# Attention and channel mix on one core: four batches instead of two turned on TensorE, a fourth output buffer, a new written order

## The chip, the core and the metric

The kernel runs on one core of a Trainium2 chip. The metric is the device time of one execution in microseconds. Before the change the median of three runs is 286.31 us (286.21 to 286.6). Five engines work side by side, each in its own written order: TensorE (PE in the profile; its weight loads PEld), VectorE (DVE), ScalarE (ACT), GpSimd (POOL), and SyncE (SP), which here issues every DMA. They wait for each other through semaphores.

## What is computed

Eight batches of eight heads, 576 tokens, 64 channels per head. First attention with a mask by blocks of 64 tokens, then a channel mix in which each token is blended with the token before it:

```python
scores = scale * np.matmul(q, k.transpose(0, 1, 3, 2))
mask = block_i >= block_j                       # blocks of 64 tokens
attn = exp(where(mask, scores, -1e9) - max)     # rows then divided by their sum
x = (attn @ v) -> (B, S, H * D)
xk = mu_k * x + (1.0 - mu_k) * x_prev           # x_prev: x one token earlier
xr = mu_r * x + (1.0 - mu_r) * x_prev
k = np.maximum(xk @ w_k, 0.0)                   # 512 -> 1024
v = k * k @ w_v                                 # 1024 -> 512
out = sigmoid(xr @ w_r) * v
```

## The kernel before

**Tasks and order.** The kernel lists some 1,370 tasks, each bound to one engine (or to one of several, which the string `PLACE` chooses), and then emits them in the sequence of the string `ORDER`. A number in `ORDER` is a task; "+n" after it puts n matmuls on the identity (L270, read by nobody) ahead of a TensorE task. So the order on every engine, and on SyncE's DMA queue, is written out by hand, and each engine runs its list strictly from front to back. A task that waits holds everything behind it on its engine. Buffers are rings with fixed sizes in `RINGS`: a task that takes a buffer waits until the last reader of its former content is done. Among them are "ld" (8, loads of queries, keys and weights), "qkt" (2, turned queries and keys of a batch), "m" (2 banks of PSUM, t_m), "mm" (2 banks of PSUM, t_mm), "s" (2, scores) and "o" (3, output tiles t_o).

**Attention of a batch.** Scores need queries and keys with channels on the partitions, and there are two ways to get them. Batches below `LONGS`, here two, take the *long* way (`add_long`, `add_long_qkt`): one DMA brings two heads, each partition reading a row of nine tokens (2304 bytes); a cast to bf16 by GpSimd, VectorE or ScalarE; groups of nine turning matmuls on TensorE (L391) into a bank t_m; and a copy out of it into t_qkt by ScalarE or VectorE. The other batches take the *DMA* way (`add_qk`): a load of two heads by token rows (256 bytes) in two DMAs (L242), a cast into NB, a tail with the last 64 tokens, loaded and cast by itself, and a DMA transpose (L322) that turns one pair of heads into t_qkt. The scores of a pair are matmuls from t_qkt (L503); exponentials on ScalarE (L525) write t_e; memsets put zeros where the mask cuts (L533); products with values and with ones (L585) go into t_m, four heads at a time; VectorE transposes and inverts the sums and multiplies (L606 to L650) into XT, channels on partitions.

**Channel mix.** Over all tokens there are nine chunks of 512. For each, blends on VectorE and ScalarE or GpSimd (L669 to L704), eight groups of four matmuls with w_k (L732) with rectifier (L744, L746) and square (L754, L756), four groups with w_r (L771) and tanh on ScalarE (L779), four groups of eight matmuls with w_v (L798), the output multiply on VectorE (L809) from t_t and t_mm into t_o, and a store of t_o (L817). The multiply takes one of the three buffers t_o, so it waits for the store three multiplies earlier to land. Channel mix of early batches is interleaved with attention of later ones.

**Queue.** Loads, tail loads, DMA transposes and stores all stand in SyncE's one list. A DMA transpose waits there for its casts, and what stands behind it waits too.

Of the kernel before, what the change touches and what calls it, by code (L numbers as in the profile page):

```python
# [10 lines left out]
BF = mybir.dt.bfloat16  # L11
AF = mybir.ActivationFunctionType
ALU = mybir.AluOpType

LONGS = 2

ORDER = """
0 3 5 7 9 11 4 13 6 17 69+88 8 73 70 15 10 74 173 71+18 12 75 72 19 14 76
85+11 97 86 81 77 53 82 16 98 25 88+9 78 18 174 89 100+11 87 83 27 79 84 101
113+2 23 20 80 90 114 109+11 102 99 21 110 94+11 115 116 26 189 28 95 121+11  # L20
112 111 127+3 122 96 169 125 24 131 126 106+7 1 123 124 54 91+3 22 31 107
128+9 39 129 92 132 37 108 133 103 170 175 117+2 104 93 2 65 134 118 55 105
135 136 40 130+28 32 171 119 120 149 38 138+2 183 137 142 139+5 181 154 151
140+2 143 152 177 176 144 179 156 145 172 29 66 153 146 158 195+31 56 147 67
182 196 197+7 185 184 178 198 199+7 200 150 209+7 35 211 210 155 205 30 45
212 201+2 206 47 180 202 141+11 213 33 68 157 207 289 214 148 36 49 208 159
203+17 215 46 57 204 48 186 160 61 216+20 190 41 34 220 164 217 187 163 165
50 221+30 219 168 43 967 167 222 191 58 973 218 62 162 42 968 223 290 974
969 970 188 166 161 975 976 224 59 44 193 971 226 977 972 314 988 225 192
978 227 985 51 989 230 228 229 63 979 60 291 990 320 194 232 231 986 980 247  # L30
315 233 292 987 982 251 235 234 248 981 298 250 64 252 236 237 238 52 983
253 310 294 321 993+2 239 254 984 997 304 241 240 255 257 249 994 242 293
296 274 243 998 256 995 244 295 1005 277 269 246 245 275 996 322 271 259 276
272 308 258 297 1006 1008 300 299 262 302 263 270 264 324 323 301 1009 1002
325 265 309 327 423 266 326 311 312 261 303 1003 260 313 328 268 305 991 306
267 999 992 307 273 278 284 279 280 1004 283 285 1007 281 1011 402 286 1000
282 1023 403 1012 329 1024 421 1014 333 1013 330 1026 287 316 288 1015 331
334 332 1025 1016 1032 318 335 1027 404 1020 337 1028 431 336 1033 422 339
1021 338 1034 407 1029 429 317 424 340 425 1039 427 343 1022 341 319 1030
345 342 344 417 1040 360 1031 346 361 364 435 1017 348 347 365 405 366 363  # L40
367 1018 350 351 428 432 349 411 430 1041 352 368 370 362 415 436 354 1019
353 356 1037 1042 369 409 355 357 382 1049 387 524 358 359 383 384 385 371
1038 1010 416 406 372 1001 388 1046 375 408 410 1050 412 373 413 426 1047
1035 418 376 389 377 1043 1036 419 1048 378 420 390 379 437 380 374 1044 438
414 1052 386 381 440 392 391 1045 441 395 528 397 396 394 393 1051 398 518
442 401 1055 400 443 1053 433 399 446 1058 444 445 529 439 540 447 1056 1059
1057 1067 1060 448 534 1061 1068 450 449 542 1076 1062 434 451 1070 1069
1077 1054 541 452 536 1078 1063 1079 1071 535 453 544 1064 1080 543 455 1065
454 1072 516 1073 456 1066 473 515 537 1074 458 457 477 1075 474 546 459 475
478 479 1087 461 460 480 522 517 545 463 481 482 519 530 538 464 520 462 532  # L50
476 465 495 521 547 1085 1088 467 466 497 469 1096 498 523 468 1089 496 470
539 483 531 1086 471 472 526 484 1097 525 533 485 500 488 550 489 486 490
551 491 527 1083 502 553 552 501 1093 493 1084 631 503 492 554 1081 629 1094
487 499 1082 504 641 555 505 494 1090 510 559 1098 508 556 628 511 513 630
560 647 512 632 1091 1129 561 558 642 514 643 1125 1130 507 562 563 509 1127
637 645 506 1126 565 564 557 1128 1099 635 648 566 651 1105 1100 569 548 568
567 1117 644 1101 653 633 1106 571 570 1118 659 586 574 1107 1108 636 590
1119 1095 575 1120 572 638 1092 549 634 1109 577 1121 576 573 654 639 587
1122 1110 589 660 578 741 591 1102 592 593 580 646 579 582 1114 594 1103 596
583 1111 1104 581 1115 640 613 588 585 1112 584 597 595 649 1113 663 614  # L60
1116 598 616 664 601 1140 756 602 666 603 665 604 748 608 600 667 605 1141
599 760 607 650 1123 610 609 1131 652 1124 612 615 606 749 1142 1134 617
1132 623 762 761 611 1137 764 744 618 624 1135 626 1133 621 668 1138 661
1167 669 622 742 763 619 1173 672 1168 670 673 1139 627 1174 620 1143 754
674 671 625 662 1161 752 1144 657 676 675 1146 1145 743 1162 750 678 677
1147 746 1149 1163 682 745 1136 1164 1148 679 655 658 1150 684 755 747 1165
1158 687 758 680 757 681 1171 685 1151 751 766 699 1159 1166 688 656 690 689
1172 753 703 1160 700 691 1152 704 686 705 683 693 692 706 759 695 701 696
694 707 767 1155 708 1153 765 697 702 698 1154 1156 721 710 709 776 867 714
1157 711 722 777 712 726 869 1175 715 779 729 778 716 727 770 717 780 781  # L70
723 1181 772 785 1176 868 718 728 782 1177 719 713 863 870 1182 784 786 783
771 720 1169 787 873 724 1178 725 789 788 730 857 731 1170 790 736 791 1179
854 1184 734 795 732 1180 737 874 740 855 792 796 1187 739 773 1185 793 768
797 1188 794 735 1205 871 1189 733 875 800 1199 1206 798 801 812 774 738 856
887 1208 1200 816 858 1183 877 1190 859 802 861 769 1209 1207 803 1201 876
1193 860 804 1191 775 1210 813 806 1192 815 878 1194 808 817 805 807 818
1196 1195 799 819 809 1202 872 820 822 862 811 814 810 1203 864 839 823 865
821 1186 1197 889 827 866 824 1198 890 840 826 1213 892 1204 879 891 834
1222 893 1214 828 836 883 837 835 1211 829 1223 885 894 830 1212 1219 895
842 1224 880 831 833 898 888 896 884 841 881 897 899 1220 825 900 886 1217  # L80
1221 832 902 901 1228 1218 903 882 904 1229 1215 908 1230 1225 838 905 909
843 1216 906 907 849 844 910 1226 925 1227 850 913 926 845 929 1231 911 853
915 1234 930 914 847 1232 931 848 916 1235 932 1249 1236 1233 917 1246 933
912 919 852 921 918 851 927 1250 1247 928 922 1251 934 1259 935 1248 923
1237 947 1260 920 1243 948 1238 950 949 1252 1239 1244 1245 924 1240 846
1253 952 937 1241 936 1254 1242 1255 953 1261 940 1256 941 1269 955 1262 942
954 943 1263 944 1270 1271 938 1264 939 945 1265 1257 946 1266 951 1258 956
957 962 1272 1267 958 1268 965 963 966 1275 1273 964 1293 1274 1276 960 959
1290 1294 1277 1278 1291 1295 961 1303 1292 1279 1296 1304 1280 1281 1297
1298 1284 1282 1287 1283 1285 1286 1305 1288 1289 1299 1306 1316 1300 1313  # L90
1317 1318 1307 1314 1315 1301 1308 1310 1309 1302 1345 1311 1319 1312 1346
1334 1320 1321 1331 1335 1340 1336 1332 1333 1322 1341 1342 1328 1323 1324
1325 1329 1337 1330 1326 1327 1343 1338 1339 1347 1344 1354 1348 1351 1355
1356 1357 1352 1353 1349 1358 1360 1359 1350 1363 1361 1362 1364 1365
"""

PLACE = (
    "PPAPDPPPPPPDDPADPDPPDAPAPAADDAAAAAAAADDDDPPPDDPDPDPDPDPDDAADDDADAPDPAA"
    "AADADDAADDAAPPDPDDPDDDDDDPDPAPDAADAAPAPPDDPDDDDPAPPPDDPPDPPPPPPDPDAPAD"
    "APPDDDDDAPDDDAAPDPDDDPPPDDPDPPDPDAADPPDAAAAPDPDAADAPPPDDDPPDPDPPPPDPPA"  # L100
    "AAAAAAPPPPDDPADADDPPDPDDDDDPPPPPDDDDADPAPDAAPDPDPPPDPDPAPDPPPPDPDPDPDD"
    "PPPDPAPDAAAAAAAPPDDPAAPDDPPPDPPDDDPPDDPDDDAPAAAADPDPAPAPDPDDDDAPADDDDD"
    "DPAPDAAADPDADDDAAAAADPDPAPDDAADADADADDADDPADAADADPAPDAAADDAAAPAADDDDAD"
    "ADAAADAPAADAAPADADAPAPADADAPADADADADADAPADAPADAD"
)


class Plan:

    def __init__(self, rings):
        self.rings = {n: [k, []] for n, k in rings.items()}
        self.tasks = []

# [27 lines left out]
def kernel(  # L144
# [26 lines left out]
    assert S == 576 and D == 64 and C == 512  # L171
    ISQ = float(1.0 / (D ** 0.5))
    PSUM = bass.MemoryType.PSUM

    RINGS = {"ld": 8, "vl": 4, "nl": 4, "nb": 4, "tl": 1, "qkt": 2, "e": 4,
             "xt": 2, "tt": 1, "rc": 2, "rt": 2, "d": 2, "xk": 3, "xr": 2,
             "kr": 3, "k2": 1, "t": 3, "o": 3, "s": 2, "m": 2, "mm": 2,
             "vo": 2, "el": 2}
    plan = Plan(RINGS)
    pools = {}  # L180
    for n, bufs in RINGS.items():
        if n in ("vo", "el", "nb", "xt"):
            continue
# [40 lines left out]
    for i in range(2):  # L224
        nc.vector.memset(VOs[i][D:P, 4], 0.0)
        nc.vector.memset(E4s[i], 0.0)
    for nb in NBs:
        nc.gpsimd.memset(nb[D:P, :, 4], 0.0)

# [170 lines left out]

                def ev(eng, me, y=y, n=n, take=take):
                    qkt = tiles["qkt", b]
                    if take:
                        nc.gpsimd.memset(qkt[:, :, 1, S:KP], 0.0)
                    pst = tiles["pq", b, g, y, n][:, :].bitcast(BF)
                    convert(eng, qkt[:, 2 * g + y, n, 0:S].rearrange(
                                "q (p j) -> q p j", j=JT),
# [504 lines left out]
```

## Time and profile before

| | |
|---|---|
| median of three runs | 286.31 us (286.21 to 286.6) |
| profiled execution | 286.77 us |
| its span, first to last instruction | 285.0 us |
| mean granted clock of TensorE | 0.975 |
| PE / DVE / ACT / POOL busy | 267.1 / 214.7 / 202.4 / 81.5 us |
| DMA queue | 50.88 MB in 137,072 packets, 81.8% of 16 engines |
| DMA transposes | 24, median 4.8 us from issue to landing |
| identity matmuls (L270) | 367, 26.8 us |

Shares are averages over a span whose stages differ: DMA is busy to about 215 us and nearly idle after, and the identity matmuls lie before 42 us. In a line of the timeline the bracket names the idle time of the engine just before and what ended it. A line of windows has, for a stretch, its length, the busy time of PE, PEld, DVE, ACT and POOL, the granted clock of TensorE, the DMA share and GB/s.

### The profile page before, as it was taken

To read this page: it belongs to the slowest core of one execution; us is meant where nothing else is said; L and a number is where in the kernel's file an instruction comes from. 1 tells how busy PE (TensorE), PEld (TensorE's weight loads), DVE (VectorE), ACT (ScalarE), POOL (GpSimd) and SP (SyncE) were. 2 spreads that over 40 slices of the span, in tenths; PEclk is the share of its full clock that TensorE was granted. 3 is DMA by queue.
4 is the path that set the end of the run, shared out by engine and by line. 5 is a ranking of instruction groups with operands and counts; after the bars stand their busy time and mean duration, and the time that the engine had idled before them with its cause. 6 is when DMAs were issued, how large, how long until landed. Compare 5 with 4: busy or idle time off the path is not lost.

```text
span 285.0 us, 8296 instructions
## 1 busy us (share of the span) xinstructions
PE 267.1 (94%) x3351; PEld 132.7 (47%) x3351; DVE 214.7 (75%) x468; ACT 202.4 (71%) x296; POOL 81.5 (29%) x161
## 2 busy tenths in 40 slices
PE   8999999998599977999999989989999999999995
PEld 8866773443234422434444434433454444444443
DVE  1448899798578893598888888999996898952432
ACT  2799599964289365987989599979967991461530
POOL 4421334723053011430163028222133212150110
PEclk9999999999699995999999999999999999999999
DMA  7979899999949998979999999999998201202103
GB/s 219 301 181 335 252 290 247 221 169 201 236 89 195 215 256 207 217 152 180 237 229 155 209 251 227 183 225 234 194 198 183 77 2 39 110 0 96 54 29 118
DMA packets 137110, 51.40 MB, mean 180 GB/s; under 512 B 127728, under 2 KB 127984, under 8 KB 137072
## 3 DMA queue, kind: packets, MB, share of 16 engines
q1 hardware_dynamic: 137072, 50.88, 81.8%
q8 instruction: 26, 0.43, 0.6%
q14 instruction: 12, 0.10, 0.1%
HBM read 33.56 MB, written 9.44 MB: 151 GB/s over the span
## 4 chain that ended last, share of the span: by engine, by line
PE 34%; ACT 15%; DMA 9%; DVE 7%; SPq 6%; issue 3%; POOL 0%; ACTq 0%; DVEq 0%
PE t_mm L732 13%; PE t_mm L798 9%; ACT t_e L525 7%; PE t_mm L771 5%; SPq L242 4%; PE t_m L585 4%; DMA t_qkt<-NB 4%; DMA out_dram<-t_o 3%; PE t_s L503 3%; DVE t_o L809 2%; ACT t_d L669 2%; ACT t_kr L744 2%; SPq L322 2%; DMA t_ld<-in_k_dram 1%; ACT NB L253 1%
## 5 line engine op out<-in xcount | busy, mean ns | idle before, releaser
L525 ACT ACTIVATE t_e<-t_s 128x1024 f16<-128x1024 f32 x96 | 94.2, 1023 | 9.6 <-PE t_s L503 9.5
L732 PE MATMUL t_mm<-t_xk,WK 128*128 128x512 f16 x288 | 73.1, 397 | 7.1 <-DVE t_o L809 6.0
L798 PE MATMUL t_mm<-WV,t_k 128*128 128x512 f16 (+1 forms) x296 | 66.9, 374 | 0.0
L732 PEld LDWEIGHTS <-WK 128*128 128x128 f16 x288 | 27.0, 100 | 44.0 <-issue 19.0
L779 ACT ACTIVATE t_t<-t_mm 128x512 f32<-128x512 f32 x36 | 21.3, 600 | 31.3 <-PE t_mm L771 29.5
L798 PEld LDWEIGHTS <-t_k 128*128 128x128 f16 x296 | 27.9, 98 | 32.7 <-issue 2.2
L809 DVE SCALAR_TENSOR_TENSOR t_o<-t_t,t_mm 128x512 f32<-128x512 f32 (+1 forms) x37 | 24.7, 668 | 22.5 <-PE t_mm L798 12.8
L756 POOL TENSOR_TENSOR t_k<-t_kr 128x512 f16<-128x512 f32 x23 | 25.3, 1104 | 48.8 <-ACT t_kr L744 32.3
L503 PE MATMUL t_s<-t_qkt 64*128 64x64 bf16 (+4 forms) x384 | 34.0, 282 | 3.9 <-DMA t_qkt<-NB 2.3
L771 PE MATMUL t_mm<-WR,t_xr 128*128 128x512 f16 x144 | 36.3, 380 | 1.0 <-DVE t_o L809 1.0
L533 POOL MEMSET t_e<- 64x128 f16 x68 | 13.1, 200 | 69.9 <-ACT t_e L525 57.8
L744 ACT ACTIVATE t_kr<-t_mm 128x512 f32<-128x512 f32 x44 | 26.3, 598 | 8.4 <-PE t_mm L732 8.3
L585 PE MATMUL t_m<-t_e,VO 128*32 128x64 f16 (+4 forms) x1024 | 29.5, 248 | 0.6 <-DVE t_tt L606 0.6
L270 PE MATMUL t_mm<-identb 128*128 128x128 bf16 x367 | 26.8, 227 | 1.4 <-POOL identb masks.py:199 1.4
L746 DVE TENSOR_SCALAR t_kr<-t_mm 128x512 f32<-128x512 f32 x28 | 19.2, 686 | 10.0 <-PE t_mm L732 9.8
L756 DVE TENSOR_TENSOR t_k<-t_kr 128x512 f16<-128x512 f32 x28 | 20.4, 734 | 7.5 <-ACT t_kr L744 7.1
L503 PEld LDWEIGHTS <-t_qkt 64*128 64x128 bf16 x384 | 13.4, 95 | 26.8 <-issue 18.3
L270 PEld LDWEIGHTS <-identb 128*128 128x128 bf16 x367 | 22.0, 102 | 4.7 <-issue 2.6
L585 PEld LDWEIGHTS <-VO 128*32 128x32 f16 x1152 | 17.8, 95 | 12.5 <-issue 7.1
L650 DVE TENSOR_TENSOR XT<-t_m,t_rt 128x512 f32<-128x512 f32 x32 | 21.7, 684 | 0.8 <-PE t_m L585 0.7
L259 POOL CAST NB<-t_ld 128x512 bf16<-128x512 f32 x20 | 13.9, 700 | 24.3 <-DMA t_ld<-in_q_dram 21.0
L771 PEld LDWEIGHTS <-t_xr 128*128 128x128 f16 x144 | 12.6, 97 | 17.1 <-issue 4.7
(59 smaller groups left out, 302.0 us busy)
## 6 DMA issues: line engine op xcount, KB each, us to landing
out_dram<-t_o SPq DMA_DIRECT2D x35, 256.0 KB, 3.0
t_vl<-in_v_dram SPq DMA_DIRECT2D x32, 256.0 KB, 4.9
t_ld<-in_q_dram SPq DMA_DIRECT2D x48, 128.0 KB, 3.7
t_ld<-in_k_dram SPq DMA_DIRECT2D x48, 128.0 KB, 3.4
t_ld<-in_q_dram SPq DMA_DIRECT2D x8, 288.0 KB, 4.9
t_ld<-in_k_dram SPq DMA_DIRECT2D x8, 288.0 KB, 5.7
t_ld<-in_moe_w_v_dram SPq DMA_DIRECT2D x8, 256.0 KB, 5.8
t_ld<-in_moe_w_k_dram SPq DMA_DIRECT2D x8, 256.0 KB, 5.0
```

The source lines that it names most:

```text
L270: nc.tensor.matmul(spare.get("at", dst), identb, identb, start=True, stop=True)
L503: nc.tensor.matmul(PS[:, h, col:col + n], qkt[rows, pr, 1, kc * P:kc * P + P], qkt[rows, pr, 0, q0:q0 + n], start=True, stop=True)
L525: nc.scalar.activation(tiles["e", b, pr][:, :, i, :], tiles["ps", b, it], AF.Exp, scale=ISQ)
L585: nc.tensor.matmul(PA[j * QC:(j + 1) * QC, col + a - lo:col + hi - lo], weight(b, (g, j), kc, kk), moving(b, (g, j), kc, a, hi), start=(kc ...
L650: nc.vector.tensor_tensor(xt[:, 2 * g + "AB".index(kind), 1:1 + CH], PA[:, 0:CH], rt_[:, 0:CH], ALU.mult)
L732: nc.tensor.matmul(ps, WK[:, cc, jc * P:(jc + 1) * P], tiles["xk", c][:, cc], start=(cc == 0), stop=(cc == CCn - 1))
L744: nc.scalar.activation(kt, ps, AF.Relu)
L756: (nc.vector if eng == "DVE" else nc.gpsimd).tensor_tensor(dst, KR, KR, ALU.mult)
L771: nc.tensor.matmul(ps, tiles["xr", c][:, cc, jt * P:(jt + 1) * P], WR[:, cc], start=(cc == 0), stop=(cc == CCn - 1))
L779: nc.scalar.activation(tiles["t", c, jt], tiles["pr", c, jt], AF.Tanh, scale=0.5)
L798: nc.tensor.matmul(ps[:, 0:w], tiles["k2", c][:, jc, jt * P:(jt + 1) * P], WV[:, jc, cols], start=(jc == 0), stop=(jc == JCn - 1))
L809: nc.vector.scalar_tensor_tensor(tiles["o", c, jt, half][:, 0:w], tiles["t", c, jt][:, cols], 1.0, tiles["pv", c, jt, half][:, 0:w], ALU.a ...
```

## The change

`LONGS` goes from 2 to 4: batches 2 and 3 are loaded by nine-token rows and turned on TensorE, and only batches 4 to 7 use the DMA transposes. The ring "o" has four buffers. The pads of the two t_qkt buffers, 64 columns that nobody else writes on the long way, are set to zero once at the start on GpSimd, instead of in the first copy of each long batch. `ORDER` and `PLACE` are new throughout.

```diff
-LONGS = 2
+LONGS = 4
 
 ORDER = """
-0 3 5 7 9 11 4 13 6 17 69+88 8 73 70 15 10 74 173 71+18 12 75 72 19 14 76
...
+0 3 5 13 7 4 9 6 17 69+64 43 73 70 74 15 8 19 10 71+39 75 72 11 44 76 85+11
...
 PLACE = (
-    "PPAPDPPPPPPDDPADPDPPDAPAPAADDAAAAAAAADDDDPPPDDPDPDPDPDPDDAADDDADAPDPAA"
...
+    "PPDDPDDPDPAPDAAPPADPPDADAAADADADADAAAADADDPPDDPDPPPPDDDDPDAAPAAAAAPAAD"
...
@@ RINGS @@
-             "kr": 3, "k2": 1, "t": 3, "o": 3, "s": 2, "m": 2, "mm": 2,
+             "kr": 3, "k2": 1, "t": 3, "o": 4, "s": 2, "m": 2, "mm": 2,
@@ start @@
+    for _ in range(RINGS["qkt"]):
+        nc.gpsimd.memset(new("qkt", [P, HP, 2, KP], BF)[:, :, 1, S:KP], 0.0)
     for nb in NBs:
         nc.gpsimd.memset(nb[D:P, :, 4], 0.0)
@@ add_long_qkt, ev @@
                     qkt = tiles["qkt", b]
-                    if take:
-                        nc.gpsimd.memset(qkt[:, :, 1, S:KP], 0.0)
                     pst = tiles["pq", b, g, y, n][:, :].bitcast(BF)
```

What the two written orders hold, counted by task, where they differ:

| | before | after |
|---|---|---|
| loads by nine-token rows (one DMA each) | 16 | 32 |
| loads by token rows (two DMAs each) | 48 | 32 |
| tail loads (two DMAs each) | 6 | 4 |
| DMA transposes | 24 | 16 |
| turning groups on TensorE (nine matmuls) | 16 | 32 |
| copies out of t_m into t_qkt: ScalarE, VectorE | 8, 8 | 17, 15 |
| identity matmuls | 367 | 401 |
| rectifiers: ScalarE, VectorE | 44, 28 | 50, 22 |
| squares: ScalarE, VectorE, GpSimd | 21, 28, 23 | 19, 26, 27 |

## Prediction

> **What bounds the kernel now.** I read the page first: engine shares, the forty slices, the list of costly groups. Then the waits, then the timeline around the two largest gaps of TensorE, then a table of windows.
>
> ```profile
> span 285.0 us, 8296 instructions
> PE 267.1 (94%) x3351; PEld 132.7 (47%) x3351; DVE 214.7 (75%) x468; ACT 202.4 (71%) x296; POOL 81.5 (29%) x161
> PE   8999999998599977999999989989999999999995
> PEclk9999999999699995999999999999999999999999
> DMA  7979899999949998979999999999998201202103
> L525 ACT ACTIVATE t_e<-t_s 128x1024 f16<-128x1024 f32 x96 | 94.2, 1023 | 9.6 <-PE t_s L503 9.5
> L732 PE MATMUL t_mm<-t_xk,WK 128*128 128x512 f16 x288 | 73.1, 397 | 7.1 <-DVE t_o L809 6.0
> t_qkt<-NB SPq DMA_TRANSPOSE x24, 4.8
> ```
>
> TensorE is busy 94% of the span, so the end is set by its work and its gaps. The gaps are few: the slices show the clock fall twice, in slices 11 and 16, and group L732 says why: 6.0 of its 7.1 us of idle time ended with L809, the output multiply on VectorE. The DMA row is full up to slice 30 and then nearly empty, so loads, stores and DMA transposes fill the queue for three quarters of the span.
>
> The view of waits gives the same chain in two links, an output buffer that waits for a store and TensorE that waits for the output multiply:
>
> ```profile
> PE t_mm L732 <- DVE t_o L809: 6.0, 2, 3.7
> DVE t_o L809 <- DMA out_dram<-t_o: 4.9, 3, 2.9
> ```
>
> The timeline of both places (start, us, engine) shows what held the store: it stands on SyncE's queue behind the DMA transposes (L322), which wait for their casts.
>
> ```profile
> 65.58 3.94 SPq L322 DMA_TRANSPOSE t_qkt<-NB  x2
> 69.56 1.18 SPq L817 DMA_DIRECT2D out_dram<-t_o  x2
> 73.36 0.69 DVE L809 SCALAR_TENSOR_TENSOR t_o<-t_t,t_mm 128x512 f32<-128x512 f32 x1 [2.87 <-DMA out_dram<-t_o]
> 74.10 1.86 PE L732 MATMUL t_mm<-t_xk,WK 128*128 128x512 f16 x4 [3.71 <-DVE t_o L809]
> ...
> 99.85 3.11 SPq L322 DMA_TRANSPOSE t_qkt<-NB  x2
> 105.10 0.26 PE L503 MATMUL t_s<-t_qkt 64*128 64x64 bf16 x6 [1.15 <-DMA t_qkt<-NB]
> 108.62 1.87 PE L732 MATMUL t_mm<-t_xk,WK 128*128 128x512 f16 x4 [2.27 <-DVE t_o L809]
> ```
>
> The windows (span, busy us of PE, PEld, DVE, ACT, POOL, granted clock, DMA share, GB/s) price what follows a gap, and cut the span in stretches that I use below:
>
> ```profile
> 75.00:80.00 5.00, 5.00 (x25) 1.75 (x25) 3.21 (x8) 2.10 (x3) 0.88 (x2) 0.55 1.14 227
> 110.00:115.00 5.00, 5.00 (x20) 1.75 (x19) 2.07 (x4) 3.41 (x5) 1.24 (x2) 0.63 0.90 218
> 5.00:10.00 5.00, 5.00 (x106) 4.69 (x104) 0.75 (x1) 1.91 (x4) 1.69 (x4) 1.00 0.98 348
> 40.00:60.00 20.00, 19.45 (x285) 9.56 (x282) 17.69 (x42) 19.42 (x29) 9.99 (x14) 1.00 1.10 233
> 42.30:128.10 85.80, 76.51 (x878) 32.45 (x877) 67.36 (x151) 60.91 (x89) 27.49 (x50) 0.92 0.99 201
> 128.10:285.00 156.90, 150.50 (x1679) 68.45 (x1677) 121.41 (x254) 110.09 (x166) 39.64 (x73) 1.00 0.71 147
> ```
>
> After each gap TensorE works at about half clock: at 0.55 and 0.63 of it in five full us.
>
> **The change part by part.** The sum stands against the profiled execution: 286.77 us, of which 285.0 are the span and 1.77 lie around it. The median of the runs is 286.31, so 0.46 lower. I cut the span at 42.3 (first matmul of L732) and 128.1 (last exponential of the fourth batch).
>
> *Fourth output buffer, and stores that are not held.* The stalls cost: at 70 us a gap of 3.7, a shorter one of 0.5, and 5.45 us of work at half clock (2.7 lost): 6.9. At 105 us gaps of 0.35, 1.15 and 2.27 and 5 us at half clock (2.5): 6.3. Together 13.2. In the written order of before, at these two places the store stands 0.9 and 1.2 us of TensorE work ahead of the multiply that takes its buffer again. In the new order with four buffers the smallest such distance while loads are running is 4.1 us (last store of chunk 3), the next 9.4, and batches 2 and 3 have no DMA transposes at all. I take both stalls as gone. What is late next is ScalarE, below.
>
> *Loads of batches 2 and 3.* Removed: 16 loads in two DMAs each (1.17 us of queue, the median in the timeline), 2 tail loads (1.33), 8 DMA transposes (1.73): 35 us of SyncE's queue, which is back to back from 41 to 214 us. Added: 16 single loads at 0.43: 7 us. The bytes of queries and keys stay, 4.7 MB, and 2.6 MB of transposes go. At 233 GB/s (40 to 60 us) the old 7.3 MB are 31 us; at 348 (5 to 10 us, when long rows are loaded) the new 4.7 are 14. So queue and DMA engines have 17 to 28 us less to do. None of it is on TensorE's path by itself; it shows as fewer late loads.
>
> *TensorE.* Added are 16 groups of nine turning matmuls. Two groups in a row take 0.60, a single one 0.43, less 0.17 of overlap: 0.21 to 0.26 each, 3.4 to 4.2 us (6.9 if none overlaps; I take 3.4), all of them after the first L732. A group waits for two casts and for one of the two banks t_m, which the copies out free; scores, L585 and L732 queue behind it. Fill matmuls are 401, not 367; 23 of the 34 lie ahead of 42.3, at 0.056 us 1.3, and two score tasks fewer stand there (1.0). So the first stretch is 42.3 + 0.3 = 42.6 (bounds 41 to 45, as the loads come in another order).
>
> *ScalarE.* Nine more copies of turned blocks (0.54 back to back), seven of them up to the last exponential of the fourth batch. In that stretch the order also puts there two exponentials (0.90 each back to back: two take 1.94, one 1.02), three long casts (0.57), three value and two weight casts (0.5), one narrow exponential (0.5), and takes away four items of 0.5. That is 3.8 + 1.8 + 1.7 + 2.5 + 0.5 - 2.0 = 8.3 more. From the window row: 60.9 + 8.3 = 69.2 us of ScalarE. TensorE in the same stretch: 76.5 less 5.2 of half clock is 71.3; four groups of L732 fewer (0.86), one of L771, two of L798 (1.73), two of L585 (0.66) and sixteen turning groups and 11 fills more: 71.3 - 4.1 = 67.2. Before, the stretch without its stalls was 72.6, which is 1.3 over its longer engine. Now two engines are nearly equal, and each runs in order; I take 2.8 over the longer one: 69.2 + 2.8 = 72.0, bounds 69.2 and 82 (the old share, 72.6 us for 60.9 of ScalarE, on 69.2).
>
> *The rest.* What the stretch no longer does comes later: 4 of L732 (3.5), 1 of L771 (0.9), 2 of L798 (3.5), 2 of L585 (1.3): 9.1. The rest was 156.9; with 9.1 it is 166.0. It had 6.4 idle, and its matmuls of L732 take 0.94 instead of 0.86 start to start. With 14 DMA transposes instead of 15 here but 17 instead of 24 split loads, and transposes issued 9 to 38 us of TensorE work ahead of their scores (4 to 22 before), I take 3.0 of it back, bounds 0 and 8: 163.0.
>
> *Pads.* Two memsets of 0.32 on GpSimd move to the start, behind those that end at 2.44; GpSimd waits until 3.79 for the first load, so they cost nothing, and 0.6 if that load came at once. VectorE has slack: ten fewer tail casts, seven more copies, six fewer rectifiers net to some 3 us less of 214.7.
>
> Sum: 42.6 + 72.0 + 163.0 = 277.6, and 1.8 around it: 279.4; less 0.46, 278.9. That is 7.4 us under the profiled execution, 2.6%.
>
> The median issue of a transpose is 1.73 us for 0.33 MB, of a split load 1.17 for 0.26 MB: 5.3 against 4.5 us per MB. [...]
>
> **The rivals.** *ScalarE does not hold* (faster still): the stretch is 69.2 and the late loads go entirely: 42.6 + 69.2 + 158.0 + 1.8 - 0.5 = 271. For it: the larger distances above. Against: in 40 to 60 us ScalarE is already busy 19.4 of 20.
>
> *The stall only moves*: one store or transpose is late again once, with its half clock: 278.9 + 6.6 = 285.5, no real change. For it: 16 transposes remain. Against: the distances.
>
> *Slower*: the copies out of turned blocks stand in ScalarE's full queue, two banks t_m serve both turning and L585, and TensorE, behind a turning group of batch 2 or 3 (45 to 75 us), waits. A wait with its half clock costs some 6.6; two make 278.9 + 13.2 = 292. From 7.4 us of such waits on it decides. For it: 69.2 against 67.2, and ScalarE's windows at 5.0 of 5.0. Against: the new order has 0.5 to 2.3 us of TensorE work between group and copy.
>
> The second drop of the clock came after gaps of 1.15 and 2.27 us with 2 us of work between. [...]
>
> **How the numbers follow.** The forecast has 0.58, the faster rival 0.14, the moved stall 0.13, the slower one 0.11, anything else that slows 0.04. 0.2%, 0.6 us, is about what a measurement tells from no change. Faster: 0.58 + 0.14 and half of the moved stall, 0.79; same 0.06; slower 0.15. The bounds give 41 + 69.2 + 158 + 1.3 = 269.5 at the low end; the high end is the moved stall and a little, 287 (all upper bounds at once, 45 + 82 + 166 + 1.3, would be 294). Out of it are the slower cases and part of the fastest.
>
> **What would show it.** Right: no wait of L809 for a store over 1 us before 215; a granted clock of 1.00 between 45 and 215; the last exponential of batch 3 near 115 us; 16 transposes; ScalarE at 95% between 43 and 115. Wrong: TensorE waiting for turned copies or exponentials over 2.3 us, a clock of 0.5 in any window of that stretch, or a first L732 later than 45.

## The result, and the profile after

The changed kernel takes 275.08 us (median of four runs, 274.54 to 275.54), beside 286.46 us for the kernel before on the same chip. The ratio is 0.9598 with a 95% interval of 0.9573 to 0.9624: 4.0% faster. The prediction was 278.9 us, range 269.5 to 287.0. The profiled execution took 275.54 us, 11.2 less than the profiled one before; 273.8 of it is the span.

These are the lines of the page that answer those shown of before. The code has moved by one to three lines: L525 is now L526, L732 is L733, L809 is L810.

```profile
span 273.8 us, 8635 instructions
...
PE 266.4 (97%) x3529; PEld 138.5 (51%) x3529; DVE 212.9 (78%) x458; ACT 210.3 (77%) x314; POOL 85.7 (31%) x158
...
PE   7999999999999999999999999999999999999994
...
PEclk9999999999999999999999999999999999999999
DMA  7979999989999869999899989999112101103003
...
L526 ACT ACTIVATE t_e<-t_s 128x1024 f16<-128x1024 f32 x96 | 94.9, 1035 | 9.1 <-PE t_s L504 8.9
...
L733 PE MATMUL t_mm<-t_xk,WK 128*128 128x512 f16 x288 | 67.9, 379 | 0.3 <-DVE t_kr L747 0.2
```

The clock no longer falls, and TensorE's row is at nine from the second slice to the last but one. The 7.1 us of idle time ahead of L732 are 0.3 ahead of L733. The DMA row is full to slice 28, where before it was to slice 31. The windows give the two stretches that the prediction used, cut where it cut them: at the first matmul of L733 (42.2 us) and at the last exponential of the fourth batch, batch 3, which now lies at 111.8 us and not at 128.1. The columns after the length are busy us of PE, PEld, DVE, ACT and POOL, then granted clock, DMA share and GB/s.

```profile
42.20:111.80 69.60, 68.01 (x987) 33.49 (x987) 63.29 (x137) 67.59 (x103) 24.55 (x46) 1.00 0.97 228
111.80:273.80 162.00, 157.81 (x1743) 71.79 (x1741) 124.95 (x260) 112.36 (x169) 47.13 (x77) 1.00 0.59 133
```

In the first of them TensorE stood idle for 1.6 us (69.60 less 68.01), where before it was 9.3 of 85.8. The second is 5.1 us longer than before, because it took over work of the first. The queue's own row of the page is smaller, too: 48.25 MB in 109,872 packets instead of 50.88 MB in 137,072.

The view of waits for L810 has no line with a store any more (of before: 4.9 us for out_dram):

```profile
DVE t_o L810 <- PE t_mm L799: 14.4, 14, 2.2
DVE t_o L810 <- ACT t_d L670: 0.5, 1, 0.5
```

### The profile page after: what moved, and what is told of

The parts are those of the page before. It is cut to its first block, busy times and chain, and to the rows that moved or that the text cites. A ratio compares the mean times of both kernels' runs of the same rounds, so it can differ in the third digit from the quotient of the medians.

```text
span 273.8 us, 8635 instructions
## 1 busy us (share of the span) xinstructions
PE 266.4 (97%) x3529; PEld 138.5 (51%) x3529; DVE 212.9 (78%) x458; ACT 210.3 (77%) x314; POOL 85.7 (31%) x158
## 2 busy tenths in 40 slices
DMA packets 109911, 48.79 MB, mean 178 GB/s; under 512 B 98480, under 2 KB 98736, under 8 KB 109872
## 3 DMA queue, kind: packets, MB, share of 16 engines
q1 hardware_dynamic: 109872, 48.25, 72.7%
## 4 chain that ended last, share of the span: by engine, by line
PE 81%; DVE 9%; ACT 4%; issue 1%; DMA 1%; SPq 1%; POOL 0%; POOLq 0%; ACTq 0%
PE t_mm L799 20%; PE t_mm L733 19%; PE t_m L586 12%; PE t_mm L772 10%; PE t_mm L273 10%; PE t_s L504 8%; PE t_m L394 3%; ACT t_e L526 2%; DMA t_vl<-in_v_dram 1%; DVE t_kr L747 1%; DVE t_o L810 1%; DVE t_xk L701 1%; DVE t_k L757 1%; DVE t_tt L607 1%; DVE t_xr L705 1%
## 5 line engine op out<-in xcount | busy, mean ns | idle before, releaser
L526 ACT ACTIVATE t_e<-t_s 128x1024 f16<-128x1024 f32 x96 | 94.9, 1035 | 9.1 <-PE t_s L504 8.9
L733 PE MATMUL t_mm<-t_xk,WK 128*128 128x512 f16 x288 | 67.9, 379 | 0.3 <-DVE t_kr L747 0.2
L757 POOL TENSOR_TENSOR t_k<-t_kr 128x512 f16<-128x512 f32 x27 | 29.3, 1091 | 55.4 <-ACT t_kr L745 41.7
L733 PEld LDWEIGHTS <-WK 128*128 128x128 f16 x288 | 26.4, 97 | 33.7 <-issue 5.9
L745 ACT ACTIVATE t_kr<-t_mm 128x512 f32<-128x512 f32 x50 | 29.8, 606 | 10.3 <-PE t_mm L733 9.9
L810 DVE SCALAR_TENSOR_TENSOR t_o<-t_t,t_mm 128x512 f32<-128x512 f32 (+1 forms) x37 | 24.7, 669 | 15.1 <-PE t_mm L799 14.4
L504 PE MATMUL t_s<-t_qkt 64*128 64x64 bf16 (+4 forms) x384 | 33.0, 277 | 0.7 <-ACT t_e L526 0.5
L273 PE MATMUL t_mm<-identb 128*128 128x128 bf16 x390 | 28.3, 230 | 1.6 <-POOL identb masks.py:199 1.4
L273 PEld LDWEIGHTS <-identb 128*128 128x128 bf16 x401 | 25.0, 103 | 5.6 <-issue 3.2
L757 DVE TENSOR_TENSOR t_k<-t_kr 128x512 f16<-128x512 f32 x26 | 18.7, 728 | 7.8 <-ACT t_kr L745 7.7
L651 DVE TENSOR_TENSOR XT<-t_m,t_rt 128x512 f32<-128x512 f32 x32 | 21.6, 687 | 4.1 <-PE t_m L586 3.8
L705 DVE SCALAR_TENSOR_TENSOR t_xr<-t_d,MUR,XT 128x512 f16<-128x512 f32 (+7 forms) x38 | 21.5, 575 | 0.5 <-POOL t_d L673 0.3
L705 DVE SCALAR_TENSOR_TENSOR t_xk<-t_d,MUK,XT 128x512 f16<-128x512 f32 (+7 forms) x38 | 21.2, 565 | 0.1
```

The source lines that it names most:

```text
L273: nc.tensor.matmul(spare.get("at", dst), identb, identb, start=True, stop=True)
L504: nc.tensor.matmul(PS[:, h, col:col + n], qkt[rows, pr, 1, kc * P:kc * P + P], qkt[rows, pr, 0, q0:q0 + n], start=True, stop=True)
L526: nc.scalar.activation(tiles["e", b, pr][:, :, i, :], tiles["ps", b, it], AF.Exp, scale=ISQ)
L705: nc.vector.scalar_tensor_tensor(dst, dt[:, 0, lo:lo + w], (MUK1, MUR1)[n][:, cc:cc + 1], x, ALU.mult, ALU.add)
L733: nc.tensor.matmul(ps, WK[:, cc, jc * P:(jc + 1) * P], tiles["xk", c][:, cc], start=(cc == 0), stop=(cc == CCn - 1))
L745: nc.scalar.activation(kt, ps, AF.Relu)
```

## Experiments

Two explanations had to be told apart. **The stalls**: the two places where a store was held behind DMA transposes cost 13.2 us, and with them gone ScalarE sets the pace; the smaller load on SyncE's queue and on the DMA engines only makes fewer loads late. That is the explanation of the prediction. **The queue**: the stalls are a symptom of a queue and DMA engines without room, and the new order gains because there is less in them. Below, "the stretch" runs from the first matmul of L732 (L733) to the last exponential of batch 3. After the stretch all variants of the new order take the same time, 161.0 to 162.0 us; ahead of it they differ by up to 2.1 us (first L733 at 41.3 to 43.4 us). Each ratio is to the kernel before, run beside it on the same chip; its median lay between 285.8 and 287.6 us, so the ratios are the better comparison.

| kernel | median, us | ratio to before (95%) | the stretch, us |
|---|---|---|---|
| before | 286.46 | 1 | 85.8 |
| before, four output buffers | 280.97 | 0.980 (0.974 to 0.987) | 79.6 |
| before, four stores moved forward | 281.45 | 0.978 (0.972 to 0.984) | 77.6 |
| new order, two long batches | 299.78 | 1.047 (1.042 to 1.053) | 94.5 |
| after | 275.08 | 0.960 (0.957 to 0.962) | 69.6 |
| after, three output buffers | 275.12 | 0.960 (0.955 to 0.966) | 69.6 |
| after, eight unread DMA transposes more | 283.08 | 0.989 (0.983 to 0.995) | 78.8 |
| after, eight unread DMA copies more | 276.81 | 0.967 (0.961 to 0.973) | 70.0 |

### The fourth buffer alone

```diff
-             "kr": 3, "k2": 1, "t": 3, "o": 3, "s": 2, "m": 2, "mm": 2,
+             "kr": 3, "k2": 1, "t": 3, "o": 4, "s": 2, "m": 2, "mm": 2,
```

> The kernel before with the ring of output tiles at four instead of three, nothing else. Theory of the stalls: both gaps (6.9 and 6.3 us with their half clock) come from the wait for a store's landing, so most of both go: 274 to 279 us. Rival, the queue: loads and DMA transposes are late anyhow in this phase, and once TensorE no longer waits for stores it waits for loads: 281 to 286 us, with waits for t_qkt or t_ld in place of L809's.

Measured: 280.97 us (279.84 to 281.28), ratio 0.980, span 279.5. Rows of the page; the last one is the chain's shares by engine:

```profile
PEclk9999999999999999999999999999999999999999
DMA  7969899999999998999999999999994101202103
...
PE 45%; DVE 15%; DMA 14%; ACT 12%; SPq 6%; issue 4%; POOL 1%; POOLq 0%; ACTq 0%; DVEq 0%
```

And the window of the stretch:

```profile
42.30:122.00 79.70, 73.02 (x890) 31.45 (x889) 67.95 (x153) 61.33 (x90) 27.18 (x50) 1.00 1.08 218
```

The clock does not fall any more, so the two stalls are gone, but only 5.5 us come of it (3.8 to 7.4 by the interval), not 13.2. In the stretch TensorE's busy time falls by 3.5 us (76.51 to 73.02: no work at half clock), its idle time by only 2.6 (9.29 to 6.68). The DMA row has lost its dips, and the DMA share of the stretch rises from 0.99 to 1.08. The chain in order of time (start, us, what) shows what came next. First the DMAs on the chain of the kernel before, which goes back to 67 us only, up to the end of the stretch:

```profile
70.31 2.95 DMA out_dram<-t_o
...
93.82 3.15 DMA out_dram<-t_o
...
104.81 2.96 DMA out_dram<-t_o
```

And with four buffers, from 67 us on:

```profile
90.75 0.03 SPq L322
90.80 5.62 DMA t_qkt<-NB
...
102.48 5.30 DMA t_vl<-in_v_dram
...
115.06 5.30 DMA t_ld<-in_q_dram
```

Where three stores stood, a transpose and two loads now stand: 16.2 us of DMA and 6.2 us of SyncE's sequencer, beside 9.1 and 5.2 before. For comparison the chains of before and of after, in this order, from their pages:

```profile
PE 34%; ACT 15%; DMA 9%; DVE 7%; SPq 6%; issue 3%; POOL 0%; ACTq 0%; DVEq 0%
```

```profile
PE 81%; DVE 9%; ACT 4%; issue 1%; DMA 1%; SPq 1%; POOL 0%; POOLq 0%; ACTq 0%
```

DMA and SyncE's sequencer have 20% of the span with four buffers alone and 2% after the whole change. The 15% of before cannot be set beside the 20%, because the chain of before covers only 74% of the span. After the change no DMA is on the chain between 42 and 112 us. So stalls and queue are both real, and the stalls alone are about half of the 11.4 us.

### The stores moved, three buffers kept

Four stores of the kernel before were moved forward in SyncE's list. "turn 2 1" is the DMA transpose of batch 2, pair 1, "qkld" a load of queries or keys, "store 0 2 0" the store of chunk 0, tile 2. One of the four, the others (0 3 0, 1 2 0, 3 3 0) likewise:

```diff
 turn 2 1
+store 0 2 0
 qkld 3 3 1
 turn 2 3
 turn 2 2
 store 0 1 0
-store 0 2 0
 tlld 3
```

> The kernel before with its three output tiles; four stores are moved forward in the order, so that each is issued 4 to 6.5 us of TensorE work ahead of the multiply that takes its tile again. If only the store's place behind the DMA transposes made the stalls, as four tiles showed it: 280 to 282 us and a clock of 1.00. Rival, the fourth tile did more than that: 284 to 287.

Measured: 281.45 us (280.14 to 282.3), ratio 0.978, clock 1.00 all through. It is the same as with the fourth buffer, within the intervals, so either of the two takes the stalls away. The chain has DMA at 15% here, beside 14% above.

### The new order without the long loads

```diff
-LONGS = 4
+LONGS = 2
```

The order, the four buffers and the places are those of after; the DMA loads, casts and transposes of batches 2 and 3 stand where their row loads, casts and turning groups stood.

> The kernel after, but with batches 2 and 3 loaded by token rows and turned by DMA transposes as before (LONGS = 2). Four output buffers stay, and the new order is kept: each load, cast and transpose stands where its counterpart of the other way stood, a transpose some 12 tasks behind its last cast. Theory of the stalls: order and fourth buffer carry the gain: at most 278 us. Rival, the queue: 28 us more of SyncE's queue and 17 us more of DMA come back between 43 and 112 us and are not hidden: 281 to 290 us.

Measured: 299.78 us (299.12 to 300.63), ratio 1.047. Rows of the page, with the chain's shares:

```profile
PE   8999998837598089999999999999999999999995
...
PEclk9999999977689759999999999999999999999999
DMA  7999999999999995799999999998920200201103
...
PE 70%; DMA 12%; DVE 6%; ACT 4%; SPq 4%; issue 2%; POOL 0%; POOLq 0%; ACTq 0%; DVEq 0%
```

The window of the stretch, and then two lines of the waits (total us, times, longest):

```profile
42.20:137.00 94.80, 73.23 (x844) 31.27 (x844) 58.48 (x134) 65.98 (x97) 25.23 (x48) 0.87 1.03 202
```

```profile
POOL NB L258 <- DMA t_ld<-in_k_dram: 19.0, 6, 6.7
...
POOL NB L258 <- DMA t_ld<-in_q_dram: 14.2, 6, 4.5
```

The new order and four buffers without the long loads are 25 us longer than after in the stretch, and the same in the rest (161.4 to 162.0). TensorE stands idle for 21.6 us of 94.8 and the clock falls three times; GpSimd's casts wait for loads. So this order by itself is no gain: it needs the long loads. One limit of this run: an order made for four long batches is not the best for two, and two casts on ScalarE also waited 10.0 us in sum for buffers NB. It shows that the order depends on the long loads, and not that no order with two could do as well. The opposite case, four long batches in the order of before, was not run.

### After with three buffers

```diff
-             "kr": 3, "k2": 1, "t": 3, "o": 4, "s": 2, "m": 2, "mm": 2,
+             "kr": 3, "k2": 1, "t": 3, "o": 3, "s": 2, "m": 2, "mm": 2,
```

Three stores were moved forward as well, so that each stands some 6 us of TensorE work ahead of the multiply that takes its buffer again. One of them in SyncE's list (the others are 1 3 0 and 3 0 0):

```diff
 qkld 4 0 1
+store 0 2 0
 store 0 0 0
 vld 2 0
...
 qkld 4 1 1
-store 0 2 0
 vld 3 4
```

> The kernel after with three output tiles instead of four; three stores are moved forward in the order so that each is issued some 6 us of TensorE work ahead of the multiply that takes its tile again. Theory that the store's place is what counts: 275 to 277 us, no wait of L809 for a store over 1 us. Rival, the fourth tile itself is needed: one or two waits of 2 to 4 us with a half clock, 281 to 288 us.

Measured: 275.12 us (274.02 to 275.44), ratio 0.960, which is that of after; the last exponential of batch 3 ends at 112.3 us (111.8 in after). The fourth buffer is not needed in the new order once those three stores stand further ahead.

### More work on ScalarE

```diff
+    on = False
     for t in plan.order():
-        t["fn"](t["eng"], t)
+        on = on or t["key"] == "pk 0 0"
+        if t["key"] == "ex 3 3 2":
+            on = False
+        again = t["key"].split()[0] in ("v", "ev", "long")
+        for _ in range(2 if on and again and t["eng"] == "ACT" else 1):
+            t["fn"](t["eng"], t)
```

> The kernel after, in which ScalarE does 20 of its copies and casts between the first matmul of L733 and the last exponential of the fourth batch twice (10 value casts, 7 copies out of t_m, 3 long casts, each with the same result): 10.5 us more of ScalarE at 0.5 to 0.57 each. Theory that ScalarE is the bound of that stretch (69.2 us of work in 69.5): 6 to 10 us longer, 281 to 285. Rival, TensorE bounds it and ScalarE has slack: up to 3 us, 275 to 278.

Measured: 287.39 us (285.66 to 288.99), ratio 1.006, 12.3 us more than after. The 20 added copies and casts take 12.1 us by the trace, and not the 10.5 expected. From the first L733 to the last exponential of batch 3 are 81.2 us, 11.5 more than after, with ScalarE busy for 80.2 of them (67.6 of 69.6 in after); one fall of the clock to half is in it, for 3.4 to 3.8 us by the clock of 0.91 over 80 to 100 us. The windows (busy us of PE, PEld, DVE, ACT, POOL) show what set the pace:

```profile
40.00:60.00 20.00, 17.42 (x255) 9.60 (x251) 13.14 (x28) 19.22 (x31) 8.64 (x13) 1.00 0.89 252
60.00:80.00 20.00, 17.65 (x278) 9.57 (x276) 17.01 (x32) 19.84 (x31) 8.29 (x17) 1.00 0.72 176
80.00:100.00 20.00, 16.75 (x217) 7.98 (x219) 14.24 (x34) 19.78 (x31) 5.08 (x10) 0.91 0.78 178
100.00:120.00 20.00, 19.00 (x296) 8.90 (x286) 17.01 (x38) 19.71 (x32) 3.46 (x9) 1.00 0.84 166
```

ScalarE is busy 78.6 us of 80 and TensorE 70.8. So ScalarE had no room for more work. That does not show yet that less work on it would help.

### Less work on ScalarE

Ten casts of values between the first L733 and the last exponential of batch 3 were moved from ScalarE to GpSimd (letters in `PLACE`, nothing else), and in a second kernel only the six after 60 us.

> The kernel after with the ten value casts that ScalarE does between the first matmul of L733 and the last exponential of the fourth batch given to GpSimd, at the same places in the order: 5.2 us less of ScalarE there, 5.8 more of GpSimd, which is a third busy. Theory that ScalarE is the bound: TensorE's 63 to 67 us come next, so 2 to 5 us shorter, 270 to 273. Rival, TensorE bounds it as well: within 1 us, 274 to 276; or, if GpSimd's queue makes the values late, slower.

> The changed kernel with six of the ten value casts moved from ScalarE to GpSimd, only those after 60 us (the four at 47 to 50 us, beside which a VectorE cast took 3.62 us, stay where they were). ScalarE has 6 x 0.5 = 3 us less before the last exponential of batch 3. If ScalarE is the bound of the stretch and the other kernel lost only by that one slow cast, this is 1 to 3 us faster than the changed kernel, 272.5 to 274.5. If VectorE is slowed beside GpSimd's casts wherever they stand, or if TensorE at 68.0 of 69.6 us is as much the bound as ScalarE, it is at 275 or above.

The second one was compared with after, run again on the same chip.

> The changed kernel as it is, for the comparison with the other two on the same chip: 275.1 us, ratio 0.960.

Ten moved: 280.6 us (279.63 to 281.17), ratio 0.975, 5.5 us more than after. The loss is at one place. The timeline of that kernel (start, us, engine; in the bracket the idle time before and what ended it):

```profile
46.48 1.34 POOL L259 CAST VO<-t_vl 128x512 f16<-128x512 f32 x2
...
47.31 3.62 DVE L259 CAST WR<-t_ld 128x512 f16<-128x512 f32 x1
...
47.78 1.03 POOL L754 TENSOR_TENSOR t_k<-t_kr 128x512 f16<-128x512 f32 x1
...
48.77 1.88 POOL L259 CAST t_nl<-t_ld 128x576 bf16<-128x576 f32 x3
...
51.14 0.69 DVE L744 TENSOR_SCALAR t_kr<-t_mm 128x512 f32<-128x512 f32 x1
...
51.88 1.01 PE L730 MATMUL t_mm<-t_xk,WK 128*128 128x512 f16 x2 [3.29 <-DVE t_kr L744]
```

A cast of weights on VectorE takes 3.62 us there; the same cast, at 47.0 us, takes 0.41 in after. It ends at 50.93, 0.3 us after the last of GpSimd's six instructions in a row. A rectifier behind it is late, TensorE waits 3.29 us and then works at half clock (0.55 over 50 to 55 us). The stretch is 74.8 us long, 5.2 more than after, which this one wait with its half clock covers. So the first of the two kernels tells nothing on ScalarE.

Six moved, without that place: 274.6 us (274.22 to 275.12), ratio 0.959 (0.954 to 0.964); after, repeated on the same chip, has 276.21 (274.98 to 277.22) and 0.963 (0.958 to 0.969). The intervals overlap. Its window from the first L733 (41.3) to the last exponential of batch 3 (111.1):

```profile
41.30:111.10 69.80, 68.15 (x990) 33.41 (x987) 64.61 (x137) 64.99 (x98) 29.92 (x52) 1.00 0.96 229
```

ScalarE has 2.6 us less than in after (67.59) and the stretch is not shorter, 69.8 beside 69.6. In time, six moved and after repeated differ ahead of the stretch: it starts at 41.3 us in the one and at 43.4 in the other, and is 69.7 and 69.6 us long. With and without the six moved, TensorE is busy for all but 1.6 us of it. So in the changed kernel TensorE sets the length of the stretch, and ScalarE is just short enough.

### The DMA transposes put back, unread

Eight DMA transposes that nobody reads were added to after, between 47 and 79 us, as many as the change took out. They go from one buffer NB into the three others, which are idle while the long batches are worked on.

```diff
+    more = {k: i for i, k in enumerate([
+        "qt 2 0 0 1", "ex 1 2 0", "pr 0 0", "qt 2 1 0 0",
+        "ex 1 3 2", "ex 2 0 0", "sc 2 02+l", "exl 2"])}
     for t in plan.order():
         t["fn"](t["eng"], t)
+        if t["key"] in more:
+            nc.sync.dma_start_transpose(
+                out=NBs[1 + more[t["key"]] % 3].rearrange(
+                    "p n t c -> p (n t) c"),
+                in_=NBs[0][:, :, :, :].rearrange("p n t c -> p (n t c)"))
```

The buffers NB are set to zero whole at the start here, by VectorE.

> The kernel after with eight DMA transposes that nobody reads, issued on SyncE's queue between 45 and 65 us, where batches 2 and 3 would have theirs; their source and targets are the NB tiles, idle until then, set to zero by VectorE at the start in place of GpSimd's pads. Theory that the queue and the DMA engines have room in the new order: up to 2 us, 275 to 277. Rival, they have none: 8 of 1.73 us of queue and the loads behind them late, 281 to 290 us.

Then the same eight as plain copies (`dma_start` in place of `dma_start_transpose`).

> The same eight unread DMAs, at the same places between 47 and 79 us, from the same buffer into the same three buffers and of the same 0.33 MB, but plain copies and not transposes: runs of 2,560 bytes in place of 256. The eight transposes cost 12.0 us (275.1 to 287.1). Theory A, it is the transposes' own cost (the queue held 1.5 to 4.1 us by each, packets of 256 bytes): a copy holds the queue about 0.43 us as the long row loads do, 8 x 0.43 = 3.4 us, and its long runs move at up to the 348 GB/s seen while long rows are loaded; the time stays at 276 to 279. Theory B, it is the bytes: 2.6 MB more at the 233 GB/s of that stretch are 11 us of full DMA engines, and the time comes out at 284 to 288, as with the transposes.

Transposes: 287.07 us (286.19 to 288.26), ratio 1.000. Copies: 279.8 us (278.93 to 280.81), ratio 0.977. In both a cast of batch 4 on ScalarE, into a buffer NB, stood still: for 5.6 us with transposes, and for 3.9 with copies, where the profile names a store, but a copy into NB issued 1.1 us ahead of that store is as likely. The waits of the kernel with transposes:

```profile
PE t_mm L799 <- ACT t_t L780: 7.3, 1, 7.3
...
ACT NB L256 <- DMA NB<-NB: 5.6, 1, 5.6
```

That wait is the experiment's own and no part of what the change removed, so both were repeated without it: the source is now the weights WK, which nothing writes any more, NB0 is left alone, and the targets are free before batch 4 takes them. The start is that of after again.

```diff
-    more = {k: i for i, k in enumerate([
+    more = dict(zip([
         "qt 2 0 0 1", "ex 1 2 0", "pr 0 0", "qt 2 1 0 0",
-        "ex 1 3 2", "ex 2 0 0", "sc 2 02+l", "exl 2"])}
+        "ex 1 3 2", "ex 2 0 0", "sc 2 02+l", "exl 2"],
+        [1, 2, 3, 1, 2, 3, 2, 3]))
...
-                out=NBs[1 + more[t["key"]] % 3].rearrange(
+                out=NBs[more[t["key"]]].rearrange(
                     "p n t c -> p (n t) c"),
-                in_=NBs[0][:, :, :, :].rearrange("p n t c -> p (n t c)"))
+                in_=WK[:, :, :].rearrange(
+                    "p a b -> p (a b)")[:, 0:10 * P].bitcast(BF))
```

> Eight unread transposes once more, at the same places, but without what blurred the first such run: there a batch-4 cast on ScalarE waited 5.6 us for a buffer that an added transpose still used, TensorE 7.3 us for ScalarE. Here the added transposes read the weights WK, which nothing writes any more, and write the buffers NB1 to NB3 in an order that has them free again before batch 4 takes them; NB0, the first that batch 4 takes, is left alone. Theory A, SyncE's queue and the DMA engines have no room left in this stretch: 8 x 1.7 us of queue are in the way of the loads behind them, and most of the 12 us stays, 282 to 287. Theory B, the wait for the buffer was the cost: the loads have 9 us and more of TensorE work of slack, and the time is 275 to 278.

> The same with eight plain copies of 0.33 MB in place of the transposes. If the transposes' queue time and their packets of 256 bytes were what cost, this is within 1 us of the changed kernel, 275 to 276.5; if bytes cost, as much as the eight transposes beside it; if the wait for the buffer was the whole cost, both are at 275 to 278.

Transposes: 283.08 us (281.57 to 284.84), ratio 0.989 (0.983 to 0.995). Copies: 276.81 us (275.36 to 277.89), ratio 0.967 (0.961 to 0.973). Beside after's 0.960 and 0.963 the copies cost 0.4 to 0.7%, 1 to 2 us, within what the intervals allow for nothing; the transposes cost 2.6 to 2.9%, 7.5 to 8.4 us. These two kernels ran on one chip and are 6.3 us apart. Of the 12.0 us of the first run with transposes, the wait for the buffer was thus, by subtraction, about a third, and the transposes themselves the rest.

The timeline of the kernel with transposes, of SyncE, ScalarE and TensorE, shows one way on which a transpose reaches TensorE:

```profile
47.75 3.70 SPq L887 DMA_TRANSPOSE NB<-WK  x1
51.54 0.52 SPq L245 DMA_DIRECT2D t_ld<-in_moe_w_v_dram  x1
...
52.59 1.33 SPq L887 DMA_TRANSPOSE NB<-WK  x1
...
55.08 0.97 SPq L245 DMA_DIRECT2D t_ld<-in_moe_w_v_dram  x1
...
61.15 0.63 ACT L258 ACTIVATE WV<-t_ld 128x512 f16<-128x512 f32 x1 [2.74 <-DMA t_ld<-in_moe_w_v_dram]
...
62.75 0.61 PE L504 MATMUL t_s<-t_qkt 64*128 64x320 bf16 x4 [2.85 <-ACT t_e L526]
```

The added transposes hold the queue, a load of weights behind them is issued at 55.1 us, ScalarE waits for it, and TensorE for ScalarE's exponential; half clock follows (0.90 over 47 to 80 us, below). The issues of the two kinds (min, median, max ns), transposes first:

```profile
L887 SPq DMA_TRANSPOSE NB<-WK x8: 1326/1778/3696, 47.7 to 78.7; - x8
```

```profile
L887 SPq DMA_DIRECT2D NB<-WK x8: 471/730/1617, 46.9 to 69.1; - x8
```

And the window from 47 to 80 us in after, with eight transposes more, and with eight copies more:

```profile
47.00:80.00 33.00, 31.80 (x495) 16.89 (x493) 30.21 (x62) 31.97 (x49) 15.60 (x28) 1.00 0.93 241
```

```profile
47.00:80.00 33.00, 29.33 (x421) 15.23 (x419) 24.09 (x48) 26.08 (x40) 12.97 (x23) 0.90 1.08 243
```

```profile
47.00:80.00 33.00, 31.66 (x493) 16.84 (x493) 30.29 (x61) 32.10 (x48) 15.03 (x26) 1.00 1.06 301
```

The eight move 2.6 MB more, which over 33 us is 79 GB/s. With copies the DMA engines go from 241 to 301 GB/s, and the loads behind them are issued up to 3.6 us later than in after, which costs TensorE nearly nothing. With transposes the engines are as busy (1.08 beside 1.06) and move 243, and other loads are issued up to 13.5 us later; part of that comes back from TensorE, which is late itself and frees buffers later. So it is not the bytes. Whether it is the queue, held 17.0 us by the eight transposes and 7.0 by the eight copies, or the DMA engines, which moved the eight transposes in 10,496 packets, all under 512 bytes, and the eight copies in 1,152, of which 1,024 are over 2 KB, these runs do not separate. Nor was the other half of the relief, long rows in one DMA in place of split loads, put back by itself.

## Why the prediction was right, and where it was off

**Direction and size.** 278.9 was predicted, 275.1 measured, 1.4% less. By the parts of the sum:

| part | predicted | measured (profiled execution) |
|---|---|---|
| to the first matmul of L732/L733 | 42.6 | 42.2 |
| the stretch | 72.0 | 69.6 |
| the rest | 163.0 | 162.0 |
| around the span | 1.8 | 1.7 |
| to the median | -0.5 | -0.5 |

**Signs that were named.** No wait of L809 (L810) for a store, a clock of 1.00 between 45 and 215 us, 16 transposes and ScalarE at 95% between 43 and 115 us (68.7 of 72.0) all came as said. The last exponential of batch 3 came at 111.8 us, 3 ahead of the 115 that was named.

**Fourth output buffer, and stores that are not held.** The step priced both stalls at 13.2 us and took them as gone. They are gone, but alone they give about 5.5 us (2.0% with four buffers, 2.2% with four stores moved). The work at half clock is gone, 3.5 us of TensorE, but of its 9.3 us of idle time only 2.6 are, because loads and a transpose take the place of the stores on the chain. The step used 72.6 us as the length of the old stretch without its stalls; with four buffers it measured 79.6.

**Loads of batches 2 and 3.** Here a statement failed: "None of it is on TensorE's path by itself". In the kernel before the stalls came first, and behind them the queue was next. The chain after the fourth buffer, the 7.5 to 8.4 us that eight transposes cost when put back, and the copies that cost 1 to 2 show that the load on the queue matters, about as much as the stalls: of 11.4 us the stalls alone are 5.5, and the other 5.9 came with the long loads and the order made for them. No run divides these 5.9 further. The queue was not "back to back" either: between 41 and 214 us it issues nothing from 78.1 to 83.9 us, after the first stall, and from 121.4 to 124.6.

**Partly luck.** The sum put the stretch together from ScalarE's work and a margin, without a term for late loads. That came true, but only because the queue had become emptier as well, for which the prediction counted nothing in this stretch. So the 13.2 us that it gave to the stalls stood for two effects, the stalls and the queue, and the size came out near although the split was wrong.

**Transposes beside other DMAs.** The prediction set the issue of a transpose beside that of a split load, 5.3 us of queue per MB and 4.5. The split loads were the wrong thing to hold it against, since they move small packets too: 127,728 of the 137,110 packets of before are under 512 bytes, and its 24 transposes make up some 31,500 of these (1,312 each, as with the eight that were put back). Beside a copy of the same bytes in long runs the difference is larger: 1.78 us of queue at the median beside 0.73, and 7.5 to 8.4 us of time for eight beside 1 to 2.

**TensorE and ScalarE in the stretch.** ScalarE was put at 69.2 us and measured 67.6. With 2.8 us over the longer engine the step gave 72.0; the stretch measured 69.6. So of the 2.4 too much, 1.6 are ScalarE's work and 0.8 the margin. TensorE was put at 67.2; the terms that the step lists, with 3.4 us for the turning groups, give 66.2, and it measured 68.0. The groups were priced too low: the rows of turning matmuls have 11.4 us after the change and 6.0 before, so 5.4 for sixteen groups. "What is late next is ScalarE" is half right: ScalarE takes no more work without loss (11.5 us for 12.1), but with 2.6 us less on it the stretch stays as long. What is next is TensorE itself, 81% of the chain.

**The rest.** 3.0 us were taken back from 166.0, and 4.0 measured. This term, the 2.4 in the stretch and 0.4 ahead of it make up the difference of 3.8.

**What the clock reads.** The prediction put the second fall of the clock behind gaps of 1.15 and 2.27 us with 2 us of work between. The timeline has 1.25 us of work between them (105.10 to 106.35), and the clock's record falls at 106.84, when 0.5 of the 2.27 us had passed. So 2.3 us, from which on its signs count a wait of TensorE, is no limit below which a wait is harmless.

**The rivals.** "ScalarE does not hold" (271) was right on the stretch, 69.2 beside 69.6 measured, and too low in the rest: 158.0 beside 162.0, where TensorE alone is busy for 157.8. "The stall only moves" (285.5) did not come; nearest to it is the fourth buffer alone, 281, where waits for loads took the stalls' place without a half clock. "Slower" did not come: the longest wait of TensorE that is named in the stretch is 0.57 us.

## What to carry to other kernels

A stall that a trace prices at 13 us is worth that only if nothing else is full behind it: here the transfers were, and the removal of the stalls alone gave 5.5. So price a removed wait together with the next wait on the same chain, and ask of each DMA on a full queue what stands behind it. In this stretch, with a DMA share of 0.97 in after and 1.09 with the eight transposes put back (42.2 to 111.8 us in both), turning two batches on TensorE took 5.4 us of its time for sixteen groups, and eight unread DMA transposes cost 7.5 to 8.4 us.

## What was not expected of the hardware

**A VectorE cast beside GpSimd's work.** 3.62 us instead of 0.41, while GpSimd ran casts and a product back to back, in the kernel with ten casts moved. The cast begins at 47.31 us, while GpSimd casts values, and goes on past the end of that instruction and through the next ones, 3.2 us longer than the 0.41. A second case stands in after: a cast of the same size begins at 51.01 us, beside two products that keep GpSimd busy from 50.75 to 52.97, and takes 1.06 us, so it ends before they do. What sets the length, and whether GpSimd's work is the cause, these runs do not show.

**Copies beside transposes.** The same 0.33 MB costs 0.1 to 0.2 us as a copy with long runs (1 to 2 us for eight), in a stretch in which it costs about 1 us as a DMA transpose (7.5 to 8.4 us for eight).

**How long the clock stays down.** In the record of the granted clock of the kernel before, both falls go to 0.50 and last 6.83 us (from 72.71 and from 106.84 us). In other runs the windows give the length: 3.4 to 3.8 us with more work on ScalarE (0.91 over 20 us), some 24 us for the falls of the new order with two long batches together (0.87 over 94.8 us), 6.8 after TensorE's wait of 3.29 us for the slow cast (0.81 over 42 to 60 us). There the clock falls at about 50.5 us (0.55 over 50 to 55), 1.4 us before the gap ends, so 5.4 us of work run at half clock: gap and lost work are 3.29 + 2.7 = 6.0 us, nearly twice the gap. In the 3 us just ahead of a fall TensorE stood idle for 2.6 and 1.6 us in the kernel before, for 2.3 to 2.9 in the one with eight transposes (where the windows put the fall between 61.8 and 62.75 us) and for about 1.9 in the one with the slow cast. Each of these falls begins inside a gap, before the gap has its full length (3.71, 2.27, 2.85 and 3.29 us). With four buffers gaps of 1.16 and 0.50 us within 3 us brought no fall, and with the stores moved a wait of 1.8 us did not. What decides whether the clock falls these runs do not show.
